# Denominators and values of two attention groups on 64 by 32 TensorE tiles, in a fused attention and feed-forward kernel

## The chip, the cores and the metric

One core of one Trainium2 chip. The metric is the time of one execution on the device in microseconds (us), median of several runs; lower is better. The profile shows one execution; its span is 1.7 to 1.8 us shorter than the time of that execution.

## The reference

Attention over 8 batches, 12 heads, 448 positions, 64 columns a head, with q and k normalised; then a feed-forward network on the 3584 rows that come out:

```python
q_n, k_n = (rmsnorm(q, g_q), rmsnorm(k, g_k))
scores = np.matmul(q_n, k_n.transpose(0, 1, 3, 2)) / np.sqrt(64)
attn = np.exp(scores - max);  attn = attn / (sum(attn) + 1e-09)
x = np.matmul(attn, v)                 # (8, 12, 448, 64) -> (3584, 768)
h = x @ w_in                           # (3584, 2048)
out = (np.maximum(h, 0) + alpha * np.minimum(h, 0)) @ w_out
```

## The kernel before

Four heads make a group, three groups a batch, 24 groups in all. For each group the scores of 64 keys are computed in four 64 by 64 tiles of the array at once (two heads by two halves of the group), ScalarE exponentiates them, a pass with a matrix of ones gives the denominators `dn`, a pass with v gives the values `av`, ScalarE inverts the denominators as exp(-ln), and VectorE multiplies. Up (`hT`) and down (`op`) products of the network use the full array and fill TensorE between these small bursts.

In the profile `sc` are the scores, `expT` their exponentials, `av` and `avb` values, `rden` inverted denominators, `tps` transposes on TensorE, `gT` the network's middle layer, and `spin` warm-up matmuls on zeros. A *set* is the small matmuls that run side by side in the array (four of 64 by 64 before, which start 3 to 4 ns apart and take 0.19 us together); a *passage* is a change of TensorE between small tiles and the full array; the *front* is the time until the third group's denominators.

```python
def over_keys(name, y, weights, spare=False):
    pool, tag = (pss, "sc") if spare else (psa, "acc")
    acc = pool.tile([128, 2, 512], FP32, name=name, tag=tag)
    e = expT[y]
    for j in range(J):                       # 7 blocks of 64 keys
        for g in range(2):
            for par in range(2):             # four 64 by 64 tiles
                nc.tensor.matmul(
                    out=acc[ds(64 * par, 64), g, :S], lhsT=weights(g, par, j),
                    rhs=e[ds(64 * g, 64), j, par, :],
                    start=(j == 0), stop=(j == J - 1))
    return acc
def den(y):
    rden[y] = over_keys("dn", y, lambda g, par, j: ones[ds(64 * g, 64), :])
# ... log(y), invert(y): two ScalarE passes over 128 x 896
# ... attv(y): over_keys with v, then xT = av * rden on VectorE

def turn(y):                                 # kT ready for the scores
    if y >= TD:                              # transposed by DMA: gain in place
        t = qkT[y, "k"].rearrange("p j g c -> p (j g c)")
        nc.vector.tensor_scalar(out=t, in0=t, scalar1=gain[:, 0:1],
                                scalar2=None, op0=ALU.mult)
        return
    # ... y < TD: transposed on TensorE, copied by VectorE

# ... the scheduler: in each burst two or three score tiles, dn or av, then
# hT and op products; turn(y) comes after the first of these or ahead of them
# GpSimd, in program order: squares and scaling of q and k, and the issue of
# the loads of v, w_in and w_out
after(2, load_w_in, 1); after(5, load_w_in, 2); after(6, load_w_in, 3)
for c in range(4):
    at(first - 2 + c, load_w_out, c)         # first: burst of the third group
```

The softmax here doesn't subtract the row's maximum and nothing guards it: scores larger than these inputs give would overflow.

Of the kernel before, what the change touches and what calls it, by code (L numbers as in the profile page):

```python
# [21 lines left out]
def kernel(  # L22
# [12 lines left out]
    nc = tc.nc  # L35
# [13 lines left out]
    TD = min(8, NG)  # L49
# [22 lines left out]
    ones = cst.tile([128, 64], FP16, name="ones", tag="ones")  # L72
# [3 lines left out]
    idle = cst.tile([128, S], FP16, name="idle", tag="idle")  # L76
    nc.vector.memset(idle, 0.0)
# [9 lines left out]
    gT = cst.tile([128, NF, W], FP16, name="gT", tag="gT")  # L87

# [26 lines left out]
    def load_w_in(c):  # L115
        nc.gpsimd.dma_start(
            out=w_in_sb[:, :, ts(c, FB)],
            in_=moe_w_in[:, ts(c, FB)].rearrange("(k p) f -> p k f", p=128),
        )

    def load_w_out(c):
        nc.gpsimd.dma_start(
            out=w_out_sb[:, ts(c, NF // 4), :],
            in_=moe_w_out[ts(c, DF // 4), :].rearrange("(t p) m -> p t m", p=128),
        )
# [86 lines left out]
    def score(y, j):  # L212
        qT, kT = qkT[y, "q"], qkT[y, "k"]
        sc = pss.tile([128, 2, 512], FP32, name="sc", tag="sc")
        for par in range(2):
            for g in range(2):
                nc.tensor.matmul(  # L217
                    out=sc[ds(64 * g, 64), par, :S].rearrange("p (j c) -> p j c", j=J),
                    lhsT=kT[ds(64 * par, 64), j, g, :],
                    rhs=qT[ds(64 * par, 64), :, g, :],  # L220
                    start=True,
                    stop=True,
                )
        scs[y, j] = sc

    def soft(y, j):
        if j == 0:
            expT[y] = att.tile([128, J, 2, S], FP16, name="expT", tag="expT")
# [5 lines left out]
    def over_keys(name, y, weights, spare=False):  # L234
        pool, tag = (pss, "sc") if spare else (psa, "acc")
        acc = pool.tile([128, 2, 512], FP32, name=name, tag=tag)
        e = expT[y]
        for j in range(J):
            for g in range(2):
                for par in range(2):  # L240
                    nc.tensor.matmul(  # L241
                        out=acc[ds(64 * par, 64), g, :S],
                        lhsT=weights(g, par, j),
                        rhs=e[ds(64 * g, 64), j, par, :],
# [3 lines left out]
        return acc  # L248

    def den(y):  # L250
        dn = over_keys("dn", y, lambda g, par, j: ones[ds(64 * g, 64), :])
        rden[y] = dn

    def log(y):
        r = att.tile([128, 2, S], FP32, name="rden", tag="rden")
        nc.scalar.activation(out=r, in_=rden[y][:, :, :S], func=AF.Ln)  # L256
        rden[y] = r

    def invert(y):
        r = rden[y]  # L260
        nc.scalar.activation(out=r, in_=r, func=AF.Exp, scale=-1.0)  # L261

    def attv(y, spare=False, jobs=()):
        b, i = divmod(y, G)
        vv = vt[b]
        av = over_keys(
            "av", y, lambda g, par, j: vv[ds(64 * g, 64), 2 * i + par, j, :], spare
        )
        for f in jobs:
            f(y)  # L270
        if i == 0:
            xT[b] = att.tile([128, 2, G, S], FP16, name="xT", tag="xT")
        nc.vector.tensor_mul(  # L273
            out=xT[b][:, :, i, :], in0=av[:, :, :S], in1=rden[y]
        )
# [46 lines left out]
    def down(b0, t, oh, jobs=(), spare=False):  # L322
# [12 lines left out]
        if oh == 0:  # L335
            osb[b0, t] = ffn.tile([128, DM], FP32, name="osb", tag="osb", bufs=3)
# [23 lines left out]
    bursts, dens, avs, first_in, last_in = [], {}, {}, {}, {}  # L360
    m = 0
    while m < NG * J or len(avs) < NG:
        n = len(bursts)
        if len(dens) > len(avs):
            avs[n] = len(avs)
        elif len(dens) < NG and last_in.get(len(dens), n) < n:
            dens[n] = len(dens)
            if dens[n] == G - 1:
                avs[n] = G - 1
# [265 lines left out]
```

## Time and profile before

| | before |
|---|---|
| time, median | 445.1 us (445.07 to 446.26, 3 runs; 445.4 with the fourth, later run) |
| TensorE busy | 422.4 us, 95% of 443.5 |
| front, until the third group's denominators | 38.2 us, at ScalarE's pace (busy 25.5 of 27.0 us from 13 to 40 us) |
| first down product | 72.7 us |

The groups of instructions that the change touches (engine, operation, out<-in, form, count, then busy us and mean ns of one):

```profile
L217 PE MATMUL sc<-qT,kT 64*64 64x448 f16 x672 | 53.5, 359 | 8.2 <-ACT expT L229 4.2
...
L241 PE MATMUL av<-expT,vt 64*64 64x448 f16 x672 | 35.9, 349 | 1.8 <-ACT rden L256 1.8
...
L241 PE MATMUL dn<-expT,ones 64*64 64x448 f16 x672 | 36.0, 349 | 0.2 <-DVE gT L318 0.2
```

The waits of TensorE after 45 us, longest first (us in total, times, longest):

```profile
PE hT L290 <- DVE gT L318: 2.4, 5, 0.9
PE sc L217 <- ACT expT L229: 2.1, 2, 1.3
PE sc L217 <- DVE kT L204: 2.0, 2, 1.3
```

These are all but 0.2 us of the waits in 400 us.

### The profile page before, as it was taken

The page shows a single profiled execution, that of the slowest core. Times are in us where ns is not written, and L with a number is a line of the kernel's source. Part 1 is how long each engine was busy: PE and PEld are TensorE (multiplying, and loading weights), DVE is VectorE, ACT ScalarE, POOL GpSimd, SP SyncE. Part 2 cuts the span into 40 slices and gives each one's busy share as a digit, 9 for nine tenths or more (in the row PEclk, how much of TensorE's full clock was granted, in tenths as well). Part 3 has the DMA queues.
Part 4 walks back from the last instruction along what each step waited for, and adds up shares of the span by engine and source line. Part 5 has one row for each costly group of instructions (what it writes and reads, how often), then busy time and mean ns, then how long its engine had stood idle before and what let it go on. Part 6 is the DMA issues. An engine that isn't in the chain of part 4 may idle for free.

```text
span 443.5 us, 9091 instructions
## 1 busy us (share of the span) xinstructions
PE 422.4 (95%) x3837; PEld 228.4 (52%) x3837; DVE 206.8 (47%) x297; ACT 290.2 (65%) x401; POOL 170.8 (39%) x125
## 2 busy tenths in 40 slices
PE   6779998899999999999999999999999999999996
PEld 3344444555445555545555545545555545555563
DVE  3656654445554454454453554445553353234421
ACT  4998888667967676766875776767875767222300
POOL 5779946551554352362554352461533000000000
PEclk9999999999999999999999999999999999999998
DMA  8999999442983491870972582651732401111132
GB/s 189 232 246 245 232 252 196 120 103 60 189 160 70 128 183 42 160 144 18 204 177 60 141 166 59 161 130 32 140 78 52 62 2 38 37 35 37 35 72 71
DMA packets 60009, 52.77 MB, mean 119 GB/s; under 512 B 32688, under 2 KB 56512, under 8 KB 59968
## 3 DMA queue, kind: packets, MB, share of 16 engines
q1 hardware_dynamic: 47424, 39.27, 37.5%
q0 software_dynamic: 11808, 11.81, 16.5%
q10 hardware_dynamic: 736, 1.11, 1.1%
q8 instruction: 30, 0.49, 0.5%
q14 instruction: 11, 0.09, 0.1%
HBM read 45.62 MB, written 11.01 MB: 128 GB/s over the span
## 4 chain that ended last, share of the span: by engine, by line
PE 84%; ACT 9%; DVE 4%; DMA 1%; issue 1%; SPq 0%; ACTq 0%
PE op L326 32%; PE hT L290 19%; PE hTa L290 10%; PE sc L217 8%; PE av L241 6%; PE dn L241 6%; ACT expT L229 5%; PE opa L326 2%; ACT ah L317 2%; DMA nat<-in_k_dram 1%; PE tps L193 1%; DVE gT L318 1%; ACT rden L256 1%; DVE kT L204 1%; DVE qT L202 1%
## 5 line engine op out<-in xcount | busy, mean ns | idle before, releaser
L229 ACT ACTIVATE expT<-sc,expb 128x896 f16<-128x896 f32 x168 | 158.5, 1007 | 18.5 <-PE sc L217 17.9
L326 PE MATMUL op<-w_out_sb,gT 128*128 128x384 f16 x848 | 145.6, 326 | 0.0
L158 POOL TENSOR_TENSOR qs<-nat,rr 128x896 f16<-128x896 f32 x44 | 78.1, 1795 | 169.5 <-issue 129.9
L326 PEld LDWEIGHTS <-gT 128*128 128x128 f16 x896 | 84.6, 98 | 63.5 <-issue 10.1
L290 PE MATMUL hT<-xT,w_in_sb 128*128 128x448 f16 x528 | 112.1, 353 | 2.4 <-DVE gT L318 2.4
L290 PEld LDWEIGHTS <-w_in_sb 128*128 128x128 f16 x768 | 73.4, 98 | 73.1 <-issue 9.1
L317 ACT ACTIVATE ah<-hT,cols 128x448 f16<-128x448 f32 x88 | 55.7, 634 | 62.9 <-PE hT L290 62.8
L318 DVE TENSOR_TENSOR gT<-hT,ah 128x448 f16<-128x448 f32 x88 | 54.8, 624 | 58.4 <-ACT ah L317 58.3
L338 DVE COPY osb<-op 128x384 f32<-128x384 f32 x53 | 29.5, 557 | 97.4 <-PE op L326 96.1
L135 POOL TENSOR_TENSOR sq<-nat 128x896 f32<-128x896 f32 x44 | 73.0, 1677 | 2.4 <-DMA nat<-in_q_dram 1.4
L217 PE MATMUL sc<-qT,kT 64*64 64x448 f16 x672 | 53.5, 359 | 8.2 <-ACT expT L229 4.2
L141 DVE TENSOR_REDUCE ss<-sq 128x14 f32<-128x896 f32 x48 | 49.9, 1076 | 6.8 <-ACT sq L133 6.3
L290 PE MATMUL hTa<-xT,w_in_sb 128*128 128x448 f16 x228 | 49.3, 352 | 0.0
L317 ACT ACTIVATE ah<-hTa,cols 128x448 f16<-128x448 f32 x38 | 24.1, 633 | 37.6 <-PE hTa L290 37.6
L318 DVE TENSOR_TENSOR gT<-hTa,ah 128x448 f16<-128x448 f32 x38 | 23.7, 624 | 33.9 <-ACT ah L317 33.9
L217 PEld LDWEIGHTS <-kT 64*64 64x64 f16 x672 | 18.6, 104 | 37.7 <-issue 26.0
L241 PE MATMUL av<-expT,vt 64*64 64x448 f16 x672 | 35.9, 349 | 1.8 <-ACT rden L256 1.8
L273 DVE TENSOR_TENSOR xT<-av,rden 128x896 f16<-128x896 f32 x24 | 26.2, 1091 | 21.6 <-PE av L241 19.8
L241 PE MATMUL dn<-expT,ones 64*64 64x448 f16 x672 | 36.0, 349 | 0.2 <-DVE gT L318 0.2
L241 PEld LDWEIGHTS <-vt 64*64 64x64 f16 x672 | 20.6, 107 | 13.3 <-issue 2.6
L241 PEld LDWEIGHTS <-ones 64*64 64x64 f16 x672 | 20.9, 107 | 11.1 <-issue 0.6
L261 ACT ACTIVATE rden<-rden 128x896 f32<-128x896 f32 x24 | 22.9, 953 | 0.7
(40 smaller groups left out, 133.1 us busy)
## 6 DMA issues: line engine op xcount, KB each, us to landing
out_dram<-osb SPq DMA_DIRECT2D x54, 192.0 KB, 2.7
nat<-in_q_dram SPq DMA_DIRECT2D x46, 224.0 KB, 4.9
nat<-in_k_dram SPq DMA_DIRECT2D x46, 224.0 KB, 5.4
vt<-in_v_dram POOLq DMA_DIRECT2D x16, 336.0 KB, 7.3
w_in_sb<-in_moe_w_in_dram POOLq DMA_DIRECT2D x4, 768.0 KB, 14.1
w_out_sb<-in_moe_w_out_dram POOLq DMA_DIRECT2D x4, 768.0 KB, 19.7
nat<-in_q_dram ACTq DMA_DIRECT2D x2, 224.0 KB, 4.7
nat<-in_k_dram ACTq DMA_DIRECT2D x2, 224.0 KB, 6.3
```

What stands on the lines that cost most here:

```text
L135: nc.gpsimd.tensor_mul(out=sqf, in0=src, in1=src)
L141: nc.vector.tensor_reduce(out=ss_t[y][:, "qk".index(nm)].rearrange("p h j -> p (h j)").unsqueeze(2), in_=sqs[y, nm], axis=AXIS_X, op=ALU.add,)
L158: eng.tensor_mul(out=t.rearrange("p j h d -> p h j d"), in0=nat[y, nm], in1=rr_t[y][:, "qk".index(nm)].unsqueeze(3).broadcast_to((128, 2, ...
L217: nc.tensor.matmul(out=sc[ds(64 * g, 64), par, :S].rearrange("p (j c) -> p j c", j=J), lhsT=kT[ds(64 * par, 64), j, g, :], rhs=qT[ds(64 * ...
L229: nc.scalar.activation(out=expT[y][:, j], in_=scs[y, j][:, :, :S], func=AF.Exp, scale=QK_SCALE, bias=expb[:, 0:1],)
L241: nc.tensor.matmul(out=acc[ds(64 * par, 64), g, :S], lhsT=weights(g, par, j), rhs=e[ds(64 * g, 64), j, par, :], start=(j == 0), stop=(j == ...
L273: nc.vector.tensor_mul(out=xT[b][:, :, i, :], in0=av[:, :, :S], in1=rden[y])
L290: nc.tensor.matmul(out=hT[:, :S], lhsT=w_in_sb[:, g * G + i, ts(ft, 128)], rhs=xT[b][:, g, i, :], start=(i == 0 and g == 0), stop=(i == G ...
L317: nc.scalar.activation(out=ah, in_=hT[:, :S], func=AF.Copy, scale=alpha_sb[:, ft : ft + 1])
L318: nc.vector.tensor_max(out=gT[:, ft, ds((b & 1) * S, S)], in0=hT[:, :S], in1=ah)
L326: nc.tensor.matmul(out=op[:, :OH], lhsT=gT[:, ft, ts(t, 128)], rhs=w_out_sb[:, ft, ds(oh * OH, OH)], start=(ft == 0), stop=(ft == NF - 1),)
L338: nc.vector.tensor_copy(out=o[:, ds(oh * OH, OH)], in_=op[:, :OH])
```

## The change

On 64 by 32 tiles eight matmuls run side by side. Since the denominator needs the same number in every column of a head, 32 columns of ones a head are enough, so two groups (four pairs of heads) share one pass. Their values need two passes: even columns of v, then odd. The third group of a batch runs alone, its two column halves side by side. Scores use the same tiles. The rows of w_in are permuted in its load to match the even and odd columns. The schedule was redone: bursts, buffers (a third `expT`), the turns (`turn`: when a group's `kT` is made ready), one group more transposed by DMA, and the loads.

```diff
-        for par in range(2):                       # score
-            for g in range(2):
-                    out=sc[ds(64 * g, 64), par, :S], lhsT=kT[ds(64 * par, 64), j, g, :],
+        for c in range(2):
+            for par in range(2):
+                for g in range(2):
+                        out=sc[ds(64 * g + 32 * c, 32), par, :S],
+                        lhsT=kT[ds(64 * par, 64), j, g, ts(c, 32)],
 ...
+        if len(ys) == 2:                           # over_keys
+            heads = [(y, par, 0) for y in ys for par in range(2)]
+        else:
+            heads = [(ys[0], par, c) for par in range(2) for c in range(2)]
         for j in range(J):
+            for h, (y, par, c) in enumerate(heads):
+                for g in range(2):
+                        out=accs[g][ds(32 * h, 32), :S],
 ...
-    def attv(y, spare=False, jobs=()):
+    def attv(ys, half, spare=False, jobs=()):      # half 0, then half 1
 ...
-    after(2, load_w_in, 1)
-    after(5, load_w_in, 2)
-    after(6, load_w_in, 3)
+    after(5, load_w_in, 1)
+    after(8, load_w_in, 2)
+    after(11, load_w_in, 3)
     for c in range(4):
-        at(first - 2 + c, load_w_out, c)
+        at(first + 1 + c, load_w_out, c)           # now by halves of the output
 ...
-        turned = n in turns and turns[n] >= TD and ups_first
+        turned = n in turns and (turns[n] >= TD or turns[n] < 2 * G) and ups_first
```

More of the change, by code (lines that the diff above doesn't have):

```diff
@@ L48 @@
     FB = DF // 4
-    TD = min(8, NG)
+    TD = min(7, NG)
+    EB = 3
+    assert G == 3
     cst = ctx.enter_context(tc.tile_pool(name="cst", bufs=1))
@@ L71 @@
     nc.vector.memset(epsb, RMS_EPS)
-    ones = cst.tile([128, 64], FP16, name="ones", tag="ones")
+    ones = cst.tile([128, 32], FP16, name="ones", tag="ones")
     nc.vector.memset(ones, 1.0)
@@ L75 @@
     make_identity(nc, ident)
-    idle = cst.tile([128, S], FP16, name="idle", tag="idle")
-    nc.vector.memset(idle, 0.0)
     ident32 = cst.tile([32, 32], FP32, name="ident32", tag="ident32")
@@ L87 @@
     gT = cst.tile([128, NF, W], FP16, name="gT", tag="gT")
+    idle = gT[:, 0, :S]
+    nc.vector.memset(idle, 0.0)
     nat, sqs, qs, ss_t, rr_t, qkT, vt, xT = {}, {}, {}, {}, {}, {}, {}, {}
@@ L115, in load_w_in @@
     def load_w_in(c):
+        src = moe_w_in[:, ts(c, FB)].rearrange("(g r) f -> g r f", g=2)
+        dst = w_in_sb[:, :, ts(c, FB)].rearrange("p (g i) f -> p g i f", g=2)
+        for g in range(2):
+            nc.gpsimd.dma_start(
+                out=dst[:, g, 0:2], in_=src[g, :256].rearrange("(p e) f -> p e f", e=2)
+            )
         nc.gpsimd.dma_start(
-            out=w_in_sb[:, :, ts(c, FB)],
-            in_=moe_w_in[:, ts(c, FB)].rearrange("(k p) f -> p k f", p=128),
+            out=dst[:, :, 2], in_=src[:, 256:].rearrange("g p f -> p g f")
         )
     def load_w_out(c):
+        oh, half = divmod(c, 2)
         nc.gpsimd.dma_start(
-            out=w_out_sb[:, ts(c, NF // 4), :],
-            in_=moe_w_out[ts(c, DF // 4), :].rearrange("(t p) m -> p t m", p=128),
+            out=w_out_sb[:, ts(half, NF // 2), ds(oh * OH, OH)],
+            in_=moe_w_out[ts(half, DF // 2), ds(oh * OH, OH)].rearrange(
+                "(t p) m -> p t m", p=128
+            ),
         )
@@ L214, in score @@
         sc = pss.tile([128, 2, 512], FP32, name="sc", tag="sc")
-        for par in range(2):
-            for g in range(2):
-                nc.tensor.matmul(
-                    out=sc[ds(64 * g, 64), par, :S].rearrange("p (j c) -> p j c", j=J),
-                    lhsT=kT[ds(64 * par, 64), j, g, :],
-                    rhs=qT[ds(64 * par, 64), :, g, :],
-                    start=True,
-                    stop=True,
-                )
+        for c in range(2):
+            for par in range(2):
+                for g in range(2):
+                    nc.tensor.matmul(
+                        out=sc[ds(64 * g + 32 * c, 32), par, :S].rearrange(
+                            "p (j c) -> p j c", j=J
+                        ),
+                        lhsT=kT[ds(64 * par, 64), j, g, ts(c, 32)],
+                        rhs=qT[ds(64 * par, 64), :, g, :],
+                        start=True,
+                        stop=True,
+                    )
         scs[y, j] = sc
@@ L227, in soft @@
         if j == 0:
-            expT[y] = att.tile([128, J, 2, S], FP16, name="expT", tag="expT")
+            expT[y] = att.tile([128, J, 2, S], FP16, name="expT", tag="expT", bufs=EB)
         nc.scalar.activation(
@@ L232, in soft, with over_keys @@
         )
-    def over_keys(name, y, weights, spare=False):
-        pool, tag = (pss, "sc") if spare else (psa, "acc")
-        acc = pool.tile([128, 2, 512], FP32, name=name, tag=tag)
-        e = expT[y]
+    def over_keys(accs, ys, weights):
+        if len(ys) == 2:
+            heads = [(y, par, 0) for y in ys for par in range(2)]
+        else:
+            heads = [(ys[0], par, c) for par in range(2) for c in range(2)]
         for j in range(J):
-            for g in range(2):
-                for par in range(2):
+            for h, (y, par, c) in enumerate(heads):
+                for g in range(2):
                     nc.tensor.matmul(
-                        out=acc[ds(64 * par, 64), g, :S],
-                        lhsT=weights(g, par, j),
-                        rhs=e[ds(64 * g, 64), j, par, :],
+                        out=accs[g][ds(32 * h, 32), :S],
+                        lhsT=weights(g, y, par, c, j),
+                        rhs=expT[y][ds(64 * g, 64), j, par, :],
                         start=(j == 0),
@@ L247, in over_keys, with den, log, invert @@
                     )
-        return acc
-    def den(y):
-        dn = over_keys("dn", y, lambda g, par, j: ones[ds(64 * g, 64), :])
-        rden[y] = dn
-    def log(y):
+    def den(ys):
+        dn = psa.tile([128, 2, 512], FP32, name="dn", tag="acc")
+        over_keys(
+            (dn[:, 0], dn[:, 1]), ys, lambda g, y, par, c, j: ones[ds(64 * g, 64), :]
+        )
+        rden[ys] = dn
+    def log(ys):
         r = att.tile([128, 2, S], FP32, name="rden", tag="rden")
-        nc.scalar.activation(out=r, in_=rden[y][:, :, :S], func=AF.Ln)
-        rden[y] = r
-    def invert(y):
-        r = rden[y]
+        nc.scalar.activation(out=r, in_=rden[ys][:, :, :S], func=AF.Ln)
+        rden[ys] = r
+    def invert(ys):
+        r = rden[ys]
         nc.scalar.activation(out=r, in_=r, func=AF.Exp, scale=-1.0)
-    def attv(y, spare=False, jobs=()):
-        b, i = divmod(y, G)
-        vv = vt[b]
-        av = over_keys(
-            "av", y, lambda g, par, j: vv[ds(64 * g, 64), 2 * i + par, j, :], spare
-        )
+    def attv(ys, half, spare=False, jobs=()):
+        b, i = divmod(ys[0], G)
+        v2 = vt[b].rearrange("p h j (d e) -> p h j d e", e=2)
+        def weights(g, y, par, c, j):
+            h = 2 * (y - G * b) + par
+            if len(ys) == 1:
+                return vt[b][ds(64 * g, 64), h, j, ts(c, 32)]
+            return v2[ds(64 * g, 64), h, j, :, half]
+        if half:
+            av, accs = None, [psf.tile([128, 512], FP32, name="avb", tag="mm") for _ in range(2)]
+        else:
+            pool, tag = (pss, "sc") if spare else (psa, "acc")
+            av = pool.tile([128, 2, 512], FP32, name="av", tag=tag)
+            accs = (av[:, 0], av[:, 1])
+        over_keys(accs, ys, weights)
         for f in jobs:
-            f(y)
-        if i == 0:
+            f(ys)
+        if b not in xT:
             xT[b] = att.tile([128, 2, G, S], FP16, name="xT", tag="xT")
-        nc.vector.tensor_mul(
-            out=xT[b][:, :, i, :], in0=av[:, :, :S], in1=rden[y]
-        )
+        x, r = xT[b][:, :, i + half, :], rden[ys]
+        if half:
+            for g in range(2):
+                nc.vector.tensor_mul(out=x[:, g], in0=accs[g][:, :S], in1=r[:, g])
+        else:
+            nc.vector.tensor_mul(out=x, in0=av[:, :, :S], in1=r)
     def bank(name, spare):
@@ L335, in down @@
         if oh == 0:
-            osb[b0, t] = ffn.tile([128, DM], FP32, name="osb", tag="osb", bufs=3)
+            osb[b0, t] = ffn.tile([128, DM], FP32, name="osb", tag="osb", bufs=2)
         o = osb[b0, t]
@@ L360 @@
     bursts, dens, avs, first_in, last_in = [], {}, {}, {}, {}
+    den_at, av_at, split = {}, {}, {}
+    steps = []
+    for y in range(0, NG, G):
+        for ys in ((y, y + 1), (y + 2,)):
+            steps += [(ys, False), (ys, True)]
     m = 0
-    while m < NG * J or len(avs) < NG:
+    while m < NG * J or steps:
         n = len(bursts)
-        if len(dens) > len(avs):
-            avs[n] = len(avs)
-        elif len(dens) < NG and last_in.get(len(dens), n) < n:
-            dens[n] = len(dens)
-            if dens[n] == G - 1:
-                avs[n] = G - 1
-        three = n in dens and dens[n] >= G or n in avs and avs[n] >= G
-        count = min(3 if three else 2, NG * J - m)
-        bursts.append([divmod(m + c, J) for c in range(count)])
-        for y, j in bursts[n]:
+        while steps:
+            ys, values = steps[0]
+            if values:
+                if n in dens and ys != (G - 1,):
+                    break
+                avs[n] = ys
+                av_at.update((y, n) for y in ys)
+            else:
+                if n in avs or any(last_in.get(y, n) >= n for y in ys):
+                    break
+                dens[n] = ys
+                den_at.update((y, n) for y in ys)
+            steps.pop(0)
+        late = any(y >= G for y in dens.get(n, ()) + avs.get(n, ()))
+        bursts.append([])
+        while len(bursts[n]) < (3 if late else 2) and m < NG * J:
+            y, j = divmod(m, J)
+            if j == 0 and y >= EB and av_at.get(y - EB, n) == n:
+                if y - EB not in av_at:
+                    break
+                split[n] = min(len(bursts[n]), 2)
+            bursts[n].append((y, j))
             first_in.setdefault(y, n)
@@ L376 @@
                 last_in[y] = n
-        m += count
+            m += 1
     NB = len(bursts)
-    den_at = {y: n for n, y in dens.items()}
-    av_at = {y: n for n, y in avs.items()}
     prep, post, roots = {}, {}, {}
@@ L389 @@
     turn_at = {
-        y: max(n for n in range(first_in[y]) if n not in dens) for y in range(1, NG)
+        y: max(n for n in range(first_in[y]) if y >= TD or n not in dens)
+        for y in range(1, NG)
     }
-    turn_at[2] = av_at[0]
+    turn_at[2], turn_at[6] = 5, 17
     turns = {n: y for y, n in turn_at.items()}
@@ L397 @@
         early = y < G + 2
-        n = turn_at[y - 1] + (y == G) if early else max(d for d in dens if d <= turn_at[y] - 2)
-        at(n - (8 if early else 5), load_qk, y)
+        if early:
+            n = turn_at[y - 1] + (y == G)
+        elif y == G + 2:
+            n = den_at[G - 1]
+        elif y == 2 * G:
+            n = turn_at[y] - 2
+        elif y % G:
+            n = den_at[y - 3 if y % G == 1 else y - G]
+        else:
+            n = av_at[y - 4]
+        at(n - (6 if early else 5), load_qk, y)
         for nm in "qk":
@@ L420 @@
         ]
-        tail = len(new) if b == B - 1 else 3 if b == 0 else 2 if odd else 1
+        tail = len(new) if b == B - 1 else 4 if b == 0 else 2 if odd else 1
         periods.append((ups, carry, new[:tail]))
@@ L427, in cost @@
             0.31 + 0.19 * len(bursts[n])
-            + (1.35 if n in dens or n in avs else 0.0) + (0.9 if turns.get(n, TD) < TD else 0.0)
+            + 1.35 * ((n in dens) + len(avs.get(n, ()))) + (0.9 if turns.get(n, TD) < TD else 0.0)
         )
@@ L439 @@
         mlp = sum(u[0] for u in ups + old + new)
-        per = (mlp + sum(cost(n) for n in range(lo, hi))) / (hi - lo)
+        stop = hi
+        if b == 0:
+            stop -= len(new)
+            mlp = sum(u[0] for u in ups)
+        per = (mlp + sum(cost(n) for n in range(lo, stop))) / (stop - lo)
         clock = 0.0
@@ L459 @@
                     break
-                short = n in turns and len(gaps[n]) < 2
-                if n < hi - 1 and not short and clock + ahead > per * (n - lo + 1):
+                short = n in turns and len(gaps[n]) < 2 or u[0] < UP
+                if n < stop - 1 and not short and clock + ahead > per * (n - lo + 1):
                     break
@@ L506 @@
         after(0, scale, 1, nm)
+    after(0, square, 2, "k")
     after(0, load_w_in, 0)
-    after(0, square, 2, "k")
     for nm in "qk":
         after(2, reduce, 2, nm)
-    after(2, load_w_in, 1)
-    after(5, load_w_in, 2)
-    after(6, load_w_in, 3)
+    after(5, load_w_in, 1)
+    after(8, load_w_in, 2)
+    after(11, load_w_in, 3)
     for c in range(4):
-        at(first - 2 + c, load_w_out, c)
-    roots[4] = 2
+        at(first + 1 + c, load_w_out, c)
+    roots[3] = 2
+    since = 2
     for n in range(NB):
@@ L525 @@
             den(dens[n])
-            attv(avs[n], True, (log, invert))
-        for t in tiles[:2]:
+            attv(avs[n], 0, True, (log, invert))
+        first_tiles = tiles[: split.get(n, 2)]
+        for t in first_tiles:
             score(*t)
@@ L537 @@
             begin(3)
-        for t in tiles[:1] if wait else tiles[:2]:
+        for t in tiles[:1] if wait else first_tiles:
             soft(*t)
@@ L542 @@
         if n in avs and not lead:
-            attv(avs[n])
-        for t in tiles[2:]:
+            for half in range(len(avs[n])):
+                attv(avs[n], half)
+        for t in tiles[len(first_tiles) :]:
             score(*t)
@@ L565 @@
         spare_at, clock = [], 0.0
-        for k, (f, a) in enumerate(gaps[n][:-1]):
-            free = 2.3 if n in dens else 1.2 if n in avs else 0.1
+        taken = n + 1 in dens or n + 1 in avs
+        for k, (f, a) in enumerate(gaps[n][: -1 if taken else None]):
+            free = 2.3 if n in dens else (0.1, 1.2, 0.0)[len(avs.get(n, ()))]
+            since += 1
             if clock >= free and not turns.get(n, TD) < TD and (
-                not spare_at or k - spare_at[-1] > 2
+                since > 2 or free == 0.0 and k == 0
             ):
                 spare_at.append(k)
+                since = 0
             clock += DOWN if f is down else UP
         ups_first = gaps[n] and gaps[n][0][0] is up
-        if ups_first:
+        if ups_first and n in dens:
             for f, a in jobs.pop(n, ()):
                 f(*a)
-        turned = n in turns and turns[n] >= TD and ups_first
+        turned = n in turns and (turns[n] >= TD or turns[n] < 2 * G) and ups_first
         if turned:
@@ L586 @@
                 done += 1
+                if n in jobs:
+                    g, c = jobs[n].pop(0)
+                    g(*c)
+                    if not jobs[n]:
+                        del jobs[n]
                 if late and done == late[0][0]:
```

## The prediction

> **What bounds the kernel now.** I read the page first, by engine and by slice, then the chain that ended last.
>
> ```profile
> PE 422.4 (95%) x3837; PEld 228.4 (52%) x3837; DVE 206.8 (47%) x297; ACT 290.2 (65%) x401; POOL 170.8 (39%) x125
> ...
> PE   6779998899999999999999999999999999999996
> ...
> ACT  4998888667967676766875776767875767222300
> ...
> DMA  8999999442983491870972582651732401111132
> ...
> PE 84%; ACT 9%; DVE 4%; DMA 1%; issue 1%; SPq 0%; ACTq 0%
> ```
>
> TensorE is busy for 95% and holds 84% of the chain. The first four slices (44 us) differ: ScalarE stands at 8 or 9 tenths there, TensorE at 6 to 9. In the waits by engine, after 45 us TensorE waits for others only 6.7 us in nearly 400. So there are two parts: a front of about 41 us at ScalarE's pace, then 400 us at TensorE's pace. A busy matmul row overlaps its neighbours, so I took each cost from distances between starts, in the timeline of TensorE from 201 to 213 us (start, length, engine, line, tiles, count):
>
> ```profile
> 201.85 1.30 PE L290 MATMUL hTa<-xT,w_in_sb 128*128 128x448 f16 x6
> 202.98 1.30 PE L290 MATMUL hT<-xT,w_in_sb 128*128 128x448 f16 x6
> 204.21 0.57 PE L217 MATMUL sc<-qT,kT 64*64 64x448 f16 x8
> 204.61 1.49 PE L241 MATMUL av<-expT,vt 64*64 64x448 f16 x28
> 205.94 0.36 PE L217 MATMUL sc<-qT,kT 64*64 64x448 f16 x4
> 206.23 2.77 PE L326 MATMUL op<-w_out_sb,gT 128*128 128x384 f16 x16
> 208.84 1.30 PE L290 MATMUL hT<-xT,w_in_sb 128*128 128x448 f16 x6
> ```
>
> Six full-array matmuls take 202.98 - 201.85 = 1.13 us, 0.188 each. The 28 small matmuls of av take 205.94 - 204.61 = 1.33 us: seven sets of four, 0.190 a set. So four 64 by 64 tiles run side by side, and a set of four costs what one full matmul of 448 columns costs. From hT (202.98) to sc (204.21) are 1.23 us where six matmuls need 1.13; from sc (205.94) to op (206.23) are 0.29 us where one set needs 0.19. Each passage between full array and small tiles thus costs about 0.10 us.
>
> [...]by moving the scores to 64 by 32 too, the change avoids a second kind of passage within a burst. [...]The single records of a set here start 3 to 4 ns apart[...] no run shows eight. [...]Here a set is four loads and four matmuls in 190 ns, 24 ns each[...]; eight tiles need 12 ns each.
>
> **The change part by part.** I counted matmuls in the instruction order of both programs. Before: sc 672, dn 672, av 672, tps 112. After, with eight to a set: sc 1344, dn 896, av and avb together 1344, tps 98. The 768 up and 896 down matmuls are the same in number and size. In sets:
> - **Scores:** 672/4 = 168 sets before, 1344/8 = 168 after. Nothing gained.
> - **Values:** 168 sets before, 168 after. A pair of groups needs two passes (even columns, then odd) in place of one pass per group. A lone third group runs its 32-column halves side by side in one pass. Nothing gained.
> - **Denominators:** 168 sets before, 896/8 = 112 after: two groups share one pass, since 32 equal columns of ones now serve each head. 56 sets go, at 0.189 us: 10.6 us of TensorE. Seven of them (1.3 us) are in the front, where TensorE is not the bound; 49 x 0.189 = **9.3 us** lie on the path.
> - **ScalarE:** two passes over the denominator (logarithm, exponential) per group become two per pair. 8 of 24 go:
>
> ```profile
> 23.39 0.32 ACT L152 ACTIVATE rr<-ss,epsb 128x28 f32<-128x28 f32 x1
> 23.74 0.23 ACT L153 ACTIVATE rr<-rr 128x28 f32<-128x28 f32 x1
> 23.87 0.90 ACT L256 ACTIVATE rden<-dn 128x896 f32<-128x896 f32 x1
> 24.80 0.95 ACT L261 ACTIVATE rden<-rden 128x896 f32<-128x896 f32 x1
> 25.66 5.67 ACT L229 ACTIVATE expT<-sc,expb 128x896 f16<-128x896 f32 x6
> ```
>
> These rows (timeline of ScalarE in the front) have no idle time in brackets: ScalarE runs without a gap. Each pair costs 0.90 + 0.95 = 1.85 us. Eight make 14.8 us, but seven lie beside TensorE's work. The one in the front counts: **1.85 us**. The front keeps the same 22 exponentials ahead of the third group's denominators, and a third exponential buffer (two before) lets the pair wait for its second group.
> - **Transposes:** one group more goes by DMA in place of TensorE: 14 matmuls fewer, about 0.056 us apart by their records: **0.8 us**.
> - **Passages:** the order of instructions changes between full array and small tiles 128 times before, 144 times after, because bursts carrying denominators or values are fewer and plain ones more: 16 x 0.10 = **1.6 us more**. If eight starts spread over 25 ns in place of 11, each of 72 bursts ends about 0.014 us later: **1.0 us more**.
> - **VectorE:** the odd halves of eight pairs are multiplied from two banks, one more instruction each; VectorE is at 47%, so hidden, unless a bank is needed at once. The odd pass takes both banks that the up and down matmuls rotate through. In most batches the next down takes the spare bank; in two it follows directly and I allow one half multiply, about 0.3 us each: **0.6 us more**.
> - **Loads:** the weights' bytes are unchanged; w_in gets three issues a chunk in place of one. w_out comes by output half, so the first down, which the new order places earlier, needs half of it. The permuted rows only match the even and odd columns; they add no work.
>
> Sum: -9.3 - 1.85 - 0.8 + 1.6 + 1.0 + 0.6 = -8.7 us. Before, the stretch from 41 to 82 us holds some 6 us of stalls of TensorE (waits for expT and kT, by the timeline). With less on ScalarE and one transpose fewer there I take 1 us of it as gone: -9.7, so 445.1 - 9.7 = **435.4 us**.
>
> **The rivals.**
> - **Eight small tiles do not keep 0.19 us a set.** [...]For: no run shows eight tiles. Against: loads and matmuls of one set already follow each other within 2 ns once queued.
> - **ScalarE becomes the bound between bursts.** With denominators packed into few bursts, plain stretches have two exponentials (about 1.9 us) and two to three ah (0.63 each) beside 2.8 to 4 us of TensorE. For: those stretches are near balance. Against: ScalarE loses 14.8 us in all, and three banks cover about 3.4 us. One lost 0.4 us in each of eight batches would give 438.
> - **The front becomes bound by DMA.** DMA stands at 9 tenths for six slices. The first down moves from 72.7 us to about 62 by my count of what precedes it; if half of w_out is not there, TensorE waits 2 to 4 us, and 438 comes out. Against: half of w_out is also bytes that need not have landed.
> - **More of the front and fewer stalls.** If the retimed turns also remove most of the 6 us of stalls, 431.
>
> **Range and chances.** The arithmetic gives 435.4; the rivals push mostly upwards, by 2 to 5 us each, and the last one down by 4. Range 431 to 443. The 2% line is 436.2, close to the centre, so faster by over 2% is 0.57, within 2% is 0.36, slower 0.07, the last nearly all for tiles that do not keep their rate.
>
> **What would show it.** In the changed profile: dn by 56 should take about 1.33 us from its start to the next set's; av and avb together 2.65; the ScalarE front should have one pair of rden rows fewer and the third group's denominators (38.4 us now) should start near 36.5; gaps at passages should stay near 0.10 to 0.12. TensorE's busy time should fall by about 10 us. I am wrong if a dn of 56 takes 1.6 us or more, if waits of TensorE after 45 us pass 10 us, or if the first down waits for its weights.

## The result

The changed kernel took **452.1 us** (450.24 to 453.38, 4 runs) against 445.4 us (445.07 to 446.26). The ratio is 1.0145, with a 95% interval of 1.0101 to 1.0188. It is slower, by less than 2%, and outside the predicted range of 431 to 443. (A ratio is the mean time of one kernel's runs over that of the other's of the same rounds, so not quite the ratio of the medians.) The profiled run, at 450.24 us, is the fastest of the four: what follows explains its 5 us, not the whole 6.7 between the medians.

The page after: engines, slices (TensorE, ScalarE, TensorE's clock, DMA) and chain.

```profile
PE 417.2 (93%) x5395; PEld 216.7 (48%) x5395; DVE 211.9 (47%) x304; ACT 278.7 (62%) x385; POOL 176.1 (39%) x133
...
PE   8769894898999899989999899989999999999996
...
ACT  4997781676887578557856568558857577223300
...
PEclk9999997999999999999999999999999999999999
DMA  8999799499627761698038970596037301111122
...
PE 80%; DVE 7%; ACT 6%; DMA 5%; issue 1%; SPq 0%; POOL 0%; DVEq 0%; ACTq 0%
```

TensorE's busy time fell by 5 us (the prediction said about 10), yet the span rose by 5. The chain now holds 7% of VectorE and 5% of DMA, where it held 4% and 1%. In the seventh slice (67 to 78 us) TensorE fell to 4 tenths and its granted clock to 7 tenths (0.50 from 75.7 to 78.4 us). The waits of TensorE after 45 us name them:

```profile
PE op L359 <- DMA w_out_sb<-in_moe_w_out_dram: 6.7, 1, 6.7
PE sc L229 <- DVE kT L190: 5.4, 4, 1.5
PE sc L229 <- ACT expT L243: 3.3, 5, 1.5
PE op L359 <- DVE xT L306: 1.1, 2, 0.6
```

The matmuls themselves did what was hoped. The timeline of TensorE in a burst of a pair:

```profile
219.92 1.51 PE L257 MATMUL dn<-expT,ones 64*32 64x448 f16 x56
221.25 0.37 PE L229 MATMUL sc<-qT,kT 64*32 64x448 f16 x8
...
224.64 1.51 PE L257 MATMUL av<-expT,vt 64*32 64x448 f16 x56
225.97 1.51 PE L257 MATMUL avb<-expT,vt 64*32 64x448 f16 x56
227.29 0.37 PE L229 MATMUL sc<-qT,kT 64*32 64x448 f16 x8
```

A pass of 56 takes 221.25 - 219.92 = 1.33 us, exactly what a pass of 28 took. Both value passes take 2.65 us. Eight tiles keep 0.19 us a set, even over 112 matmuls in a row.

Sorting the distances between starts of successive matmuls in both traces into work (0.189 us a set or an up product, 0.163 a down product), passages (up to 0.117 us at each change between tiles and full array) and the rest gives where the 5 us came from:

| us, from the first matmul to the last | before | after | difference |
|---|---|---|---|
| work | 400.4 | 390.3 | -10.1 |
| passages (128, 144) | 13.0 | 15.4 | +2.4 |
| rest: TensorE stands still or runs at a reduced clock | 24.1 | 37.0 | +12.9 |
| sum | 437.5 | 442.7 | +5.2 |

The front contributes 13.3 and 13.0 us to the rest before and after; the +12.9 lie almost wholly behind it. (How the starts within a set are split moves each row by up to 3 us and the differences by one or two; their signs and order stay.)

### The profile page after: what moved, and what is told of

Read it like the earlier page. It is cut to its first block, busy times and chain, and to the rows that moved or that the text cites.

```text
span 448.5 us, 12208 instructions
## 1 busy us (share of the span) xinstructions
PE 417.2 (93%) x5395; PEld 216.7 (48%) x5395; DVE 211.9 (47%) x304; ACT 278.7 (62%) x385; POOL 176.1 (39%) x133
## 3 DMA queue, kind: packets, MB, share of 16 engines
q0 software_dynamic: 13984, 11.81, 17.5%
q10 hardware_dynamic: 736, 1.11, 1.0%
## 4 chain that ended last, share of the span: by engine, by line
PE 80%; DVE 7%; ACT 6%; DMA 5%; issue 1%; SPq 0%; POOL 0%; DVEq 0%; ACTq 0%
PE op L359 27%; PE hT L323 19%; PE hTa L323 9%; PE sc L229 7%; PE av L257 5%; PE dn L257 4%; PE opa L359 4%; DMA w_out_sb<-in_moe_w_out_dram 4%; ACT expT L243 4%; PE avb L257 2%; DVE ss L152 2%; DVE kT L190 2%; DMA nat<-in_k_dram 1%; ACT ah L350 1%; PE tps L204 1%
## 5 line engine op out<-in xcount | busy, mean ns | idle before, releaser
L243 ACT ACTIVATE expT<-sc,expb 128x896 f16<-128x896 f32 x168 | 161.3, 1004 | 48.8 <-PE sc L229 47.9
L359 PE MATMUL op<-w_out_sb,gT 128*128 128x384 f16 x784 | 136.5, 328 | 7.8 <-DMA w_out_sb<-in_moe_w_out_dram 6.7
L229 PE MATMUL sc<-qT,kT 64*32 64x448 f16 x1344 | 53.6, 354 | 13.0 <-ACT expT L243 5.9
L229 PEld LDWEIGHTS <-kT 64*32 64x32 f16 x1344 | 15.6, 89 | 43.4 <-issue 29.1
L308 DVE TENSOR_TENSOR xT<-av,rden 128x896 f16<-128x896 f32 x16 | 17.5, 1092 | 22.0 <-PE av L257 20.2
L257 PEld LDWEIGHTS <-vt 64*32 64x32 f16 x1344 | 19.6, 93 | 14.6 <-issue 3.0
L257 PE MATMUL av<-expT,vt 64*32 64x448 f16 x896 | 24.1, 349 | 0.9 <-ACT rden L274 0.9
L257 PE MATMUL dn<-expT,ones 64*32 64x448 f16 x896 | 24.1, 349 | 0.8 <-DVE kT L215 0.8
L359 PE MATMUL opa<-w_out_sb,gT 128*128 128x384 f16 x112 | 19.4, 326 | 0.0
L274 ACT ACTIVATE rden<-dn 128x896 f32<-128x896 f32 x16 | 14.8, 926 | 4.1 <-PE dn L257 4.1
## 6 DMA issues: line engine op xcount, KB each, us to landing
w_out_sb<-in_moe_w_out_dram POOLq DMA_DIRECT2D x4, 768.0 KB, 18.1
```

The costliest lines, as they stand in the source:

```text
L229: nc.tensor.matmul(out=sc[ds(64 * g + 32 * c, 32), par, :S].rearrange("p (j c) -> p j c", j=J), lhsT=kT[ds(64 * par, 64), j, g, ts(c, 32)] ...
L243: nc.scalar.activation(out=expT[y][:, j], in_=scs[y, j][:, :, :S], func=AF.Exp, scale=QK_SCALE, bias=expb[:, 0:1],)
L257: nc.tensor.matmul(out=accs[g][ds(32 * h, 32), :S], lhsT=weights(g, y, par, c, j), rhs=expT[y][ds(64 * g, 64), j, par, :], start=(j == 0), ...
L308: nc.vector.tensor_mul(out=x, in0=av[:, :, :S], in1=r)
L359: nc.tensor.matmul(out=op[:, :OH], lhsT=gT[:, ft, ts(t, 128)], rhs=w_out_sb[:, ft, ds(oh * OH, OH)], start=(ft == 0), stop=(ft == NF - 1),)
```

## The experiments

Three theories for the rest. **A, late weights:** GpSimd issued the second quarter of w_out at 59.1 us (before: 43.1), behind other work in its order, and the first down product, which the new order places earlier (67.5 us against 72.7), needed it. **C, VectorE blocked by GpSimd:** `kT` was multiplied while GpSimd was scaling q and k. **G, late instructions:** stalls marked issue in the front (1.05 us in the changed kernel), if they come from late packets of the instruction queue (42 in its profile for 10,817 records of TensorE, about one for 256). Rivals: a full DMA front that only passes the delay on (B), late transposes (D), tiles or memory instead of instruction count (H). All runs compare with the kernel before on the same chip, 4 runs of each experiment. They came in three batches on three chips; the kernel before had medians of 445.5, 445.5 and 445.4 us there. Each kernel has one profile, and the runs of one kernel differ by up to 3.6 us, so a difference between two profiles can be that of two executions.

| experiment | us, median (range) | ratio to before, 95% interval |
|---|---|---|
| e1_wout_early | 449.7 (449.07 to 451.85) | 1.0102 (1.0075, 1.0128) |
| e2_win_wout_early | 445.2 (444.93 to 446.10) | 0.9990 (0.9973, 1.0006) |
| e3_kt_first | 446.5 (444.69 to 447.70) | 1.0018 (0.9986, 1.0050) |
| e6_before_sc32 | 454.1 (454.01 to 454.92) | 1.0197 (1.0181, 1.0212) |
| e4_loads_kt | 439.9 (439.47 to 440.78) | 0.9876 (0.9858, 0.9894) |
| e5_loads_kt_order | 439.8 (439.05 to 442.64) | 0.9884 (0.9849, 0.9919) |
| e7_fixed_sc64 | 441.7 (440.95 to 444.45) | 0.9925 (0.9890, 0.9959) |
| e8_fixed_den_twice | 456.3 (454.62 to 457.52) | 1.0233 (1.0199, 1.0267) |
| e9_front_sc64 | 440.2 (439.60 to 441.06) | 0.9891 (0.9874, 0.9907) |
| e10_front_split | 440.9 (438.24 to 441.38) | 0.9888 (0.9858, 0.9918) |
| e11_front_both | 438.1 (437.11 to 440.66) | 0.9846 (0.9815, 0.9877) |
| e12_light_dma (wrong result on purpose) | 439.3 (437.99 to 440.47) | 0.9863 (0.9842, 0.9884) |

### Late weights: e1 and e2

The changed kernel around the first down product, in the timeline of TensorE (the bracket is the idle time before, and what ended it):

```profile
67.55 1.48 PE L359 MATMUL op<-w_out_sb,gT 128*128 128x384 f16 x8
75.69 2.72 PE L359 MATMUL op<-w_out_sb,gT 128*128 128x384 f16 x8 [6.66 <-DMA w_out_sb<-in_moe_w_out_dram]
```

Eight of its sixteen matmuls run on the first quarter of w_out; the other eight wait 6.66 us for the second and then run at a granted clock of 0.50, 2.72 us in place of 1.48. The quarters, now by output half, did not take longer themselves: 18.1 us from issue to landing (median), 19.7 in the kernel before.

```diff
 # e1
-        at(first + 1 + c, load_w_out, c)
+        at(first - 2 + c, load_w_out, c)
```

> The changed kernel with only the four w_out loads issued three bursts earlier (as early as in the kernel before). Theory A, late weights: in the changed kernel the second quarter of w_out was issued at 59.1 us and TensorE waited 6.7 us for it at 67.3 us, then ran some 1 us more at half clock; issued at about 42 us it lands in time, so the wait is gone and the time is 443 to 445 us. Rival B, a full DMA front: DMA is at nine tenths there, so the bytes are only reordered; the last w_in loads, now behind three w_out loads, are late instead, and TensorE waits 4 us or more for w_in: 448 to 451.

Measured 449.7: the rival's number. The wait for w_out is gone, and another stands in its place:

```profile
PE hTa L323 <- DMA w_in_sb<-in_moe_w_in_dram: 3.8, 2, 2.5
```

Three quarters of w_out went ahead of the last w_in load, which was needed first. So the DMA engines are full there (their mean share is 1.1 to 1.3 from 40 to 70 us in this run; the share adds up the packets' times, so it can pass 1), and which bytes go first matters.

```diff
 # e2
-    after(11, load_w_in, 3)
+    after(9, load_w_in, 3)
-        at(first + 1 + c, load_w_out, c)
+        at(first + (-1, -1, 3, 4)[c], load_w_out, c)
```

> The changed kernel with the last w_in load issued two bursts earlier and only the two w_out quarters that the first down needs issued right behind it (about 42 to 45 us); the other two stay late. Theory A, late issue: no wait for w_out or w_in, 442 to 445 us. Rival B, a full DMA front: the same bytes have to come before 67 us whatever the order, and a wait of 3 us or more stands somewhere before the first down: 447 or more.

Measured 445.2, some 7 us less than the change as made. The first down product no longer waits; the third and fourth quarters of w_out do cost something (0.4 and 3.2 us):

```profile
PE op L359 <- DMA w_out_sb<-in_moe_w_out_dram: 3.6, 2, 3.2
```

So A holds for most of it and B for the rest: order and time of issue were wrong by about 7 us, and some 3.6 us remained of a front that has more to load than time.

### VectorE blocked by GpSimd: e3

The changed kernel at 192 us, timeline of all engines:

```profile
193.62 3.33 POOL L169 TENSOR_TENSOR qs<-nat,rr 128x896 f16<-128x896 f32 x2 [7.24 <-ACT rr L164]
...
195.31 1.89 DVE L190 TENSOR_SCALAR kT<-kT,gain 128x896 f16<-128x896 f16 x1
...
197.26 0.38 PE L229 MATMUL sc<-qT,kT 64*32 64x448 f16 x8 [1.20 <-DVE kT L190]
```

The same multiplication takes 0.44 us where GpSimd is idle. Here it starts 0.04 us after GpSimd's second operation did (by its record) and ends 0.25 us after that one's end, and the scores wait. In the changed kernel's trace it took 0.44 us in the five places where no GpSimd operation ran, and 1.84 to 1.89 us in the five where it came 0.04 to 0.09 us after a GpSimd operation had started; in each of these it ended 0.25 us after that operation's end. In the kernel before it came, in 14 of 16 places, late in an operation and ended 0.25 us after that one's end, 0.46 to 0.67 us in all; in the other two none ran (0.44 us). What the two engines share, the traces do not show.

```diff
-        turned = n in turns and (turns[n] >= TD or turns[n] < 2 * G) and ups_first
+        turned = n in turns and (turns[n] >= TD or turns[n] < 2 * G and ups_first)
```

> The changed kernel with the multiplication of kT by the gain (groups transposed by DMA) put at the head of VectorE's work of its burst, ahead of the output copy, so that it no longer meets the running GpSimd multiplication. Theory C, VectorE blocked by GpSimd: kT takes 0.45 to 0.7 us everywhere in place of 1.9 us in four places, the 5.4 us that TensorE waits for it go, 445 to 447 us (the w_out wait stays). Rival D: kT was late because its transposed data were; VectorE now waits for the DMA at the same places and holds other work up: 449 or more.

Measured 446.5, within what C gives, and all four waits for this multiplication are gone from TensorE's list. The multiplications (shortest, median and longest, ns) in this run:

```profile
L190 DVE TENSOR_SCALAR kT<-kT,gain x17: 443/444/1396, 105.0 to 358.6; 128x896 f16<-128x896 f16 x17
```

From 140 us on, the rest of the ledger fell from 8.4 to 2.5 us. D shows once: at 105 us VectorE waited 2.9 us for a transposed kT, whose multiplication then took 1.40 us beside GpSimd, and TensorE waited 0.8 us for an output copy behind it, a wait that the changed kernel does not have.

### Eight tiles in the kernel before: e6

```diff
-        for par in range(2):
-            for g in range(2):           # four 64 by 64 score tiles
+        for c in range(2):
+            for par in range(2):
+                for g in range(2):       # eight 64 by 32 score tiles
```

> The kernel before with nothing changed but its scores on eight 64 by 32 tiles in place of four 64 by 64. Theory E: eight tiles keep 0.19 us a set, but each burst now changes between 64 by 64 and 64 by 32 up to twice, at about 0.10 us[...]; 46 bursts with denominators or values hold two such changes, so 446 to 455[...]. Rival F: instructions for eight tiles arrive too slowly: a score set then takes over 0.2 us and TensorE waits on issue.

Measured 454.1, 8.6 us more, within 446 to 455; no wait of TensorE's matmuls on issue shows, so F is out. The timeline of TensorE in one burst:

```profile
208.01 0.57 PE L218 MATMUL sc<-qT,kT 64*32 64x448 f16 x16
208.51 1.52 PE L244 MATMUL av<-expT,vt 64*64 64x448 f16 x28
209.96 0.38 PE L218 MATMUL sc<-qT,kT 64*32 64x448 f16 x8
210.28 2.77 PE L329 MATMUL op<-w_out_sb,gT 128*128 128x384 f16 x16
```

From sc to av are 0.50 us for two sets (0.38), from av to sc 1.45 for seven (1.33): 0.12 us at each. The order of instructions holds 89 such passages between scores and denominators or values, and 8.6/89 = 0.097 us. So here a change between two kinds of tile cost about what one to or from the full array did (0.09 to 0.12 us), and the change was right to move the scores too.

### The fixes together: e4, e5, and two checks on them

e4 is e2 and e3 in one kernel.

> The early weights (the second experiment, 445.2 us, 3.6 us of waits for w_out left) and the early kT multiplication (the third, whose waits for kT fell from 5.4 us to nothing) together in the changed kernel. If the two losses are separate, the time is 445.2 - 5.4 = 440 us, within 1.5. If removing one only exposes the other (both waiting on the same full DMA front), it stays at 443 or above.

Measured 439.9, as the sum of the two gains. The profiles show that this is partly luck: against e2, e4 lost the 5.4 us for kT and also the 3.6 us for w_out, but gained 3.0 us of stops marked issue in the front (4.3 against 1.3) and the 0.8 us for the output copy. e4 beats both kernels, the one before by 1.2%.

```diff
 # e5: e4, and
+        if b == 0:
+            new[1], new[2] = new[2], new[1]   # first halves of two tiles first
```

> The fourth with the first four down products in the order: first half of two tiles, then second half of both, so that the second output half of w_out is needed one burst (some 5 us) later. Theory A: the last 3.6 us of waits for w_out go, 436 to 437.5 us. Rival B, a full DMA front: something else waits there in its place and it stays near 440.

Measured 439.8: no gain. The cause shows in e4's own profile, which has no wait for w_out left. The last two quarters landed at 71.3 and 76.2 us and were first needed at 77.4, where e2 had them at 74.8 and 79.5 and wanted them from 74.5. So e4 wanted them later, since its front ended later (next section), and the last one also came sooner. This run could not tell A from B.

```diff
 # e7: e5 with score() as in the kernel before (four 64 by 64 tiles)
```

> The fifth with its scores back on four 64 by 64 tiles, denominators and values on 64 by 32. Theory E: [...] as the kernel before with 64 by 32 scores suggests (454.1 against 445.5); some 30 bursts hold two such passages, so 5 to 7 us more than the fifth. Rival: the 8.6 us there came from something else in eight-tile scores, and this kernel is as fast as the fifth or faster.

Measured 441.7, 1.8 us more than e5, less than expected, with runs from 441.0 to 444.5. Its profiled run was the slowest, and its span is 4.9 us longer than e5's. From 140 us on the ledger has 7.1 us of rest in place of 2.5, which fits the passages; its front was shorter (third denominators at 37.9 us against 41.7). The direction holds; the size stays open between 1.8 and 4.9 us.

```diff
 # e8: e5, and in den()
+        for _ in range(2 if ys[0] >= G else 1):
             over_keys((dn[:, 0], dn[:, 1]), ys, ...)
```

> The fifth with each of the last fourteen denominator passes run twice (the second pass starts anew, the result is the same): 98 sets more. If TensorE's sets lie wholly on the path at 0.189 us, 98 x 0.189 = 18.5 us more than the fifth, within 1.5. If waits elsewhere hide a part of it, less: under 14. If instructions arrive too slowly for long bursts of eight tiles, more: over 21.

Measured 456.3, 16.5 us more, half a microsecond short of what was expected for sets wholly on the path; by the profiled spans 17.5, within it. The 1.0 us that is missing there has its place: e8's front ended 1.7 us earlier than e5's, and it has a stop of 0.9 us at 345 us (next section). So a denominator set is on the path at close to 0.189 us, which was the core of the prediction's gain.

### The front: e9 to e12

e4 still lies 4.5 us above the predicted 435.4. The timeline of its front, TensorE:

```profile
32.17 0.37 PE L257 MATMUL avb<-expT,vt 64*32 64x448 f16 x3
35.03 1.51 PE L257 MATMUL avb<-expT,vt 64*32 64x448 f16 x53 [2.49 <-issue]
...
39.32 0.92 PE L257 MATMUL dn<-expT,ones 64*32 64x448 f16 x25
42.05 0.95 PE L257 MATMUL dn<-expT,ones 64*32 64x448 f16 x31 [1.82 <-issue]
```

TensorE stops in mid pass and waits for nothing that the profile shows. Counting TensorE's records (matmuls, weight loads and a few semaphore records) from the start, the stop (0.4 to 3.3 us) comes right after the 705th or the 961st in every run that has one in the front, whatever operation stands there: values, denominators, scores, transposes. e8 has one more, 0.92 us at 345 us, after its 10,177th record. These counts lie 256 and 36 x 256 apart, and the instruction queue's packets in these traces have 16,384 bytes: 42 of them in the changed kernel and 30 before, for 10,817 and 7,699 records of TensorE, about one for 256. Each stop in the front ends 1.3 to 1.6 us after such a packet has landed (32.5 and 33.8 us in the changed kernel; 33.6 and 35.0 in e4). So the stops fit a packet that comes late. The kernel before has no such stop: its packet landed at 34.6 us, and it came to its 705th record only at 40.1 us, where e4, with twice the instructions for the same set, was there at 32.2.

```diff
 # e9: e4, scores on 64 by 64 tiles in the front only: 176 instructions fewer there
+        if y * J + j < FRONT:
+            # ... four 64 by 64 tiles, as before
```

> The fourth (439.9 us) with the scores of the front alone, ahead of the third group's denominators, on four 64 by 64 tiles, so that TensorE gets 176 instructions fewer there. Theory G: the stalls marked issue in the front (2.5 and 1.8 us in the fourth), always at the 705th and 961st instruction of TensorE, are instruction blocks of 256 that come late over the full DMA engines; with fewer instructions a microsecond they shrink by 2 us or more in sum: 436 to 438. Rival H: the stalls come with the array's tiles or memory, not with the instruction count: unchanged sum, 439.5 to 442 with the added passages.

The stops fell from 4.3 to 2.1 us in sum, and moved from values and denominators to transposes and scores at the same two counts. The time did not follow: 440.2. In its profile a wait for w_out of 1.2 us and one of 1.8 us for an output copy (behind a kT that now waited for its transpose) took the place. A miss in the time. The stops fit G, but do not show it: kernels with the same TensorE instructions in the front have sums from 1.1 us (the changed kernel) over 2.7 (e3) to 4.3 (e4), and e11, with as few instructions as e9, has 2.9.

```diff
 # e10: e4, odd half of the front's pair one burst later
+                if half and n < den_at[G - 1]:
+                    held = avs[n]
+                    continue
+        elif held:
+            attv(held, 1)
```

> The fourth with the odd half of the first pair's values put one burst later in the front, behind the next scores, so that ScalarE gets two score tiles 1.3 us earlier. Theory I: in the front ScalarE stood idle 1.8 us because the scores sat behind both value passes; now it does not, and the front ends 1 to 1.8 us earlier: 438 to 439, if the stalls marked issue let it. If late instructions set the front's end whatever the order, the time stays within 0.7 us of 439.9.

Measured 440.9, from 438.2 to 441.4: inconclusive, the runs spread over more than the effect. The stop at the 705th record stayed, 2.2 us.

> The two before together: fewer instructions in the front and the odd half one burst later. Theories G and I: 435 to 437 us. If only one of the two holds, as good as that one alone.

e11 joins e9 and e10: 438.1, the lowest median of all, 1.5% under the kernel before, though stops of 0.6 and 2.3 us stood in its profiled run, which was its slowest (440.7; the others 437.1 to 438.2). It is above the 435 to 437 expected for both, and since neither change helped alone, what they do together is not explained.

```diff
 # e12: e4, wrong result on purpose
+        if c:
+            return                            # load_w_in: the first quarter only
-        lhsT=w_in_sb[:, g * G + i, ts(ft, 128)],
+        lhsT=w_in_sb[:, g * G + i, ts(ft % (NF // 4), 128)],
```

> Wrong result on purpose: the fourth with only the first quarter of w_in loaded and used in place of the other three (same instructions on TensorE, some 4.7 MB less read in the front). Theory G: with DMA less full the blocks of instructions come in time, the stalls marked issue at the 705th and 961st instruction fall below 1 us in sum, 435 to 437 us. Rival H: the stalls have nothing to do with DMA and keep their 3 to 4 us.

The stop at the 961st record vanished; the one at the 705th did not, and the time was 439.3 us, no clear gain:

```profile
PE avb L259 <- issue: 2.4, 1, 2.4
```

From 30 to 34 us the mean DMA share was 0.69 here and 1.16 in e4, and yet the first stop was as long (2.4 us, 2.5 in e4). From 26 to 30 us it was still 1.11, and when the packet is asked for is not known, so the test is not clean. Full DMA engines are not shown to be the cause of the first stop. That the stops are late instruction packets rests on the fixed counts and the landings; what makes the packets late stays open.

## Why the prediction was wrong

- **The work was right.** Predicted 56 sets (10.6 us) and 14 transposes (0.8) less, with four warm-up matmuls more (0.75) that it did not count: 10.6 in all; the ledger has 10.1. e8 shows that such sets are on the path.
- **The passages were right.** Predicted 1.6 + 1.0 us more; measured 2.4. (Between sets and the full array: 0.103 us from four tiles, 0.116 from eight, 0.093 back.)
- **The first rival (eight tiles too slow) was wrong.** A pass of 56 takes 1.33 us; av and avb are 224 instructions in 2.65 us, 12 ns each. That instructions would come too slowly for that was the guess, which no run had shown. TensorE did stop on issue in another way, in the front (1.05 us in the changed kernel).
- **The step that failed is the sum of the waits.** It was put at -1.85 (front) + 0.6 (bank) - 1.0 (stalls gone) = -2.25 us and measured +12.9. Four things failed:
  - *Loads:* dismissed as unchanged bytes; the rival "the front becomes bound by DMA" named the very wait, with 2 to 4 us, and 6.7 us of wait and about 1.2 at half clock came. It also put the first down product at 62 us; it started at 67.5.
  - *kT:* 5.4 us in four places, in no part of the prediction: it counted VectorE's load (47%) and not what GpSimd is doing at that moment. e3 removed it.
  - *The stalls taken as gone:* the prediction read some 6 us of waits for expT and kT between 41 and 82 us. The trace has 4.1, and the changed kernel still has 4.1 after 45 us (3.3 for expT, 0.8 for a kT that was transposed on TensorE).
  - *The front's gain:* the third denominators started at 38.12 us in place of the predicted 36.5 (before: 38.21, which the prediction read as 38.4). ScalarE did lose its 1.85 us of work, but then stood idle 1.79 us, because its next scores lay behind both value passes of the pair and a stop marked issue:

```profile
31.09 1.52 PE L257 MATMUL av<-expT,vt 64*32 64x448 f16 x56 [0.88 <-ACT rden L274]
32.41 0.37 PE L257 MATMUL avb<-expT,vt 64*32 64x448 f16 x3
33.84 1.51 PE L257 MATMUL avb<-expT,vt 64*32 64x448 f16 x53 [1.05 <-issue]
35.00 0.72 PE L229 MATMUL sc<-qT,kT 64*32 64x448 f16 x16
```

- **The bank wait was about right:** 0.6 us predicted, 1.1 us measured (op behind xT, twice).
- **Two of its three signs of being wrong came:** the first down product waited for its weights, and the waits of TensorE after 45 us were 18.2 us, over the 10 that it named. The dn of 56 held its 1.33 us.
- **The rival "ScalarE becomes the bound between bursts"** did not come: the waits for expT after 45 us are 3.3 us against 2.1.

With the loads and the kT multiplication put right (e4) the same tiles give 439.9, inside the predicted range; the rest to 435.4 is of the size of the front's stops (4.3 us in that run), but no run shows that it would go with them: e9 halved them and stayed at 440.2.

## What to carry to other kernels

When a change removes work from an engine that is busy 95% of the time, the arithmetic of the work is the easy part. The schedule that was tuned around the old order goes with it, so for every load ask when its issue now stands in its engine's order and when its first reader now comes (6.7 us of wait for w_out here), and for every VectorE operation ahead of a critical matmul what GpSimd is doing then (0.44 us became 1.89). Keep all small matmuls of a burst in one tiling (e6 lost 8.6 us over 89 passages), and watch for stops in mid pass that come at fixed instruction counts (4.3 us in e4, after the 705th and 961st record).
